# Reordering the first k.v products of a linear-attention and SwiGLU kernel on one core

## Chip, cores and metric

The kernel runs on one core of a Trainium2 chip. The metric is the device time of one execution in microseconds (us), as the median of several executions; lower is better. A profiled execution gives the trace that is read here. The engines are PE (TensorE, matmuls), PEld (its weight loads), DVE (VectorE), ACT (ScalarE), POOL (GpSimd, which here issues most of the loads) and SP (SyncE). "L292" is line 292 of the kernel.

## The reference

```python
def phi(x): return np.where(x > 0, x, np.exp(x) - 1.0) + 1.0
# q, k, v: [batch 8, heads 8, seq 576, dim 64]
kv  = einsum('bhsd,bhse->bhde', phi(k), v)
z   = sum(phi(k), axis=2)
num = einsum('bhsd,bhde->bhse', phi(q), kv)
den = einsum('bhsd,bhd->bhs', phi(q), z)[..., None] + 1e-06
x   = (num / den) as [4608 tokens, 512]
out = (silu(x @ w_gate) * (x @ w_val)) @ w_out        # w_gate, w_val: 512 x 1536
```

## The kernel before

phi(x) is computed as max(x, 0) + min(exp(x), 1). For k, `mx_k` writes the max to `kp`, `exp_k` and `mn_k` write the min to `ek`, and `add_k` adds `ek` into `kp`. The heads of a batch are worked on in two halves (`lp` 0 and 1). `zt` sums k over the sequence on PE, for the max and the min term in turn; `kv_corner` is the k.v product of one half, 36 small matmuls in 64 by 64 tiles; `t_corners` multiplies q by z or by k.v; `lnrd` forms 1/den as exp(-ln(den)) on ACT; `x_t` multiplies the two on DVE; `warm` issues filler matmuls on ones while PE has nothing to do.

```python
WARM = (4, 1, 4, 3, 2, 1, 1, 1)
def kv_corner(b, lp, t, first, last):
    ps = kvp[b]
    for j in range(J):                    # J = 9
        for l2 in range(2):
            for hh in range(2):
                ... nc.tensor.matmul(out=ps[hh][64 x 64 corner], lhsT=t[...], rhs=vr[...],
                                     start=(first and j == 0), stop=(last and j == J - 1))
...                                       # batch 0, the order in which all engines get their work
zt(0, 0, X[1], ek, False, True)
zr_copy(0, 0, X[1])
warm(WARM[4])
t_corners(0, Zr, 0, pp4[2])
lnrd(pp4[2], 0)
q_phi(1, 1, qb)
mn_k(0, 1)
zt(0, 1, Y[0], kp, True, False)
warm(WARM[5])
zt(0, 1, Y[0], ek, False, True)
add_k(0, 0)
zr_copy(0, 1, Y[0])
warm(WARM[6])
kv_corner(0, 0, kp, True, True)
t_corners(0, Zr, 1, Y)
lnrd(Y, 1)
r_copy(0, 0, 1, "VV")
add_k(0, 1)
t_corners(0, R, 0, X)
x_t(0, 0, X)
kv_corner(0, 1, kp, True, True)
r_copy(0, 1, 2, "VV")
warm(WARM[7], ps=pp4[2][1])
l1_mm(0, 0, pp4[2], (0,))                 # layer 1, chunk 0 of x, blocks 0 and 1
l1_mm(0, 1, X, (0,))
t_corners(0, R, 1, pp4[1])
x_t(0, 1, pp4[1])
for c in (1, 2, 3):                       # the other chunks
    l1_mm(0, 0, pp4[2], (c,))
    l1_mm(0, 1, X, (c,))
...
for t in range(4):                        # end of layer 2 of group 0, with batch 1 between
    if t == 1:
        for lp in range(2):
            kv_corner(1, lp, kp, True, True)
        r_copy(1, 0, 2, "VV")
    if t == 2:
        nx(0, dz)                         # q.kv and x of batch 1
        nx(1, cq)
    for fb in range(FO, FB):
        l2_mm(0, t, fb)
```

Every matmul is two PE instructions, a weight load and the matmul itself (the page of before has 2185 of each).

## Time and profile before

| | before |
|---|---|
| median of 3 runs | 314.12 us (313.8 to 314.37) |
| PE busy, share of the span | 98% |
| ACT begins exp of k (first half) | 8.29 us |
| first matmul of L292 (layer 1 proper) | 18.59 us |
| first layer 1 matmul of group 1 | 49.87 us |
| end of the last matmul | 309.02 us |

The trace's clock starts at the span's start. When k lands differs between executions by up to half a microsecond (ACT's first exp of k starts between 7.83 and 8.36 us in the traces of this study) and moves all that follows. So for the first stage I use the interval from that exp to the first matmul of L292: 18.59 - 8.29 = 10.30 us in the kernel before. Its two ends in the ACT and PE timelines of before (start, length, what), and the piece of the chain of waits with chunks 1 to 3 of layer 1:

```profile
8.29 1.16 ACT L120 ACTIVATE ek<-kr 128x1152 f16<-128x1152 f16 x1 [0.27 <-DMA kr<-in_k_dram]
18.59 1.03 PE L292 MATMUL pp<-xT,wg 128*128 128x512 f16 x4
```

```profile
16.01 2.74 PE pp L276 x12
```

### The profile page before, as it was taken

The page shows a single profiled execution, that of the slowest core. Times are in us where ns is not written, and L with a number is a line of the kernel's source. Part 1 is how long each engine was busy: PE and PEld are TensorE (multiplying, and loading weights), DVE is VectorE, ACT ScalarE, POOL GpSimd, SP SyncE. Part 2 cuts the span into 40 slices and gives each one's busy share as a digit, 9 for nine tenths or more (in the row PEclk, how much of TensorE's full clock was granted, in tenths as well). Part 3 has the DMA queues.
Part 4 walks back from the last instruction along what each step waited for, and adds up shares of the span by engine and source line. Part 5 has one row for each costly group of instructions (what it writes and reads, how often), then busy time and mean ns, then how long its engine had stood idle before and what let it go on. Part 6 is the DMA issues. An engine that isn't in the chain of part 4 may idle for free.

```text
span 312.4 us, 5524 instructions
## 1 busy us (share of the span) xinstructions
PE 306.1 (98%) x2185; PEld 142.3 (46%) x2185; DVE 205.0 (66%) x362; ACT 152.8 (49%) x231; POOL 48.6 (16%) x73
## 2 busy tenths in 40 slices
PE   8899999999999999999999999999999999999994
PEld 4344454444544454445444544454444444444442
DVE  4854869999599657976697859874981434143410
ACT  4955959539733845375535643475330333133311
POOL 8655445300000410032001400000000000000000
PEclk9999999999999999999999999999999999999999
DMA  8999999998412594139612990324032300140014
GB/s 215 200 196 200 206 206 236 234 206 140 108 25 41 86 198 118 38 47 188 169 31 47 140 224 4 71 47 92 0 70 58 84 1 1 42 94 0 2 34 101
DMA packets 41178, 32.80 MB, mean 105 GB/s; under 512 B 16448, under 2 KB 36160, under 8 KB 41152
## 3 DMA queue, kind: packets, MB, share of 16 engines
q0 software_dynamic: 20480, 18.29, 37.3%
q1 hardware_dynamic: 20592, 14.13, 18.9%
q8 instruction: 17, 0.28, 0.4%
q14 instruction: 9, 0.07, 0.1%
q10 hardware_dynamic: 80, 0.03, 0.0%
HBM read 37.75 MB, written 9.44 MB: 151 GB/s over the span
## 4 chain that ended last, share of the span: by engine, by line
PE 95%; DMA 2%; DVE 1%; ACT 0%; issue 0%; POOL 0%; POOLq 0%
PE pp L292 57%; PE pp L299 30%; PE pp L276 2%; DMA kr<-in_k_dram 2%; PE pp L185 2%; PE pp L254 2%; PE pp L124 0%; ACT ek L120 0%; PE pp L411 0%; DVE kp L159 0%; PE pp L212 0%; PE pp L374 0%; DVE osb L322 0%; DVE ek L147 0%; DVE R L201 0%
## 5 line engine op out<-in xcount | busy, mean ns | idle before, releaser
L120 ACT ACTIVATE sil<-pp 128x512 f16<-128x512 f32 x108 | 63.5, 597 | 101.8 <-PE pp L292 96.7
L292 PE MATMUL pp<-xT,wg 128*128 128x512 f16 x416 | 106.8, 379 | 0.0
L292 PE MATMUL pp<-xT,wv 128*128 128x512 f16 x416 | 106.8, 379 | 0.0
L285 DVE SCALAR_TENSOR_TENSOR hT<-pp,sil 128x512 f16<-128x512 f32 x108 | 72.3, 681 | 48.5 <-PE pp L292 35.5
L299 PE MATMUL pp<-wo,hT 128*128 128x512 f16 (+2 forms) x444 | 97.1, 374 | 0.6 <-DVE osb L322 0.6
L299 PEld LDWEIGHTS <-hT 128*128 128x128 f16 x444 | 42.0, 98 | 49.8 <-issue 2.1
L292 PEld LDWEIGHTS <-wv 128*128 128x128 f16 x416 | 40.7, 98 | 49.1
L292 PEld LDWEIGHTS <-wg 128*128 128x128 f16 x416 | 40.7, 98 | 48.5
L322 DVE TENSOR_SCALAR osb<-pp 128x512 f32<-128x512 f32 (+1 forms) x19 | 12.9, 681 | 31.3 <-PE pp L299 31.3
L120 ACT ACTIVATE osb<-pp 128x512 f32<-128x512 f32 (+1 forms) x18 | 10.3, 574 | 34.8 <-PE pp L299 34.8
L120 ACT ACTIVATE ek<-kr 128x1152 f16<-128x1152 f16 x16 | 17.9, 1156 | 0.3 <-DMA kr<-in_k_dram 0.3
L120 ACT ACT_TABLE_LOAD x13 | 16.7, 1283 | 2.5 <-PE pp L292 2.4
L706 POOL COPY gate<-qT 128x1 f16<-128x1 f16 x4 | 1.3, 313 | 96.5 <-DMA qT<-qp 68.5
L229 DVE TENSOR_TENSOR qp<-qp,rden 128x1152 f16<-128x1152 f16 x12 | 16.2, 1346 | 0.0
L220 DVE TENSOR_REDUCE den<-prod 128x18 f32<-128x1152 f16 x12 | 16.1, 1342 | 0.0
L120 ACT ACTIVATE eq<-qr 128x1152 f16<-128x1152 f16 (+1 forms) x15 | 15.9, 1102 | 0.0
L271 DVE TENSOR_SCALAR xT<-pp 128x512 f16<-128x512 f32 (+1 forms) x14 | 8.8, 667 | 7.2 <-PE pp L254 7.1
L103 POOL DMA_DIRECT2D vr<-in_v_dram x16 | 12.0, 752 | 8.8 <-DMA wo<-in_moe_w_out_dram 2.4
L103 POOL DMA_DIRECT2D kr<-in_k_dram x16 | 11.5, 723 | 8.4 <-DMA wo<-in_moe_w_out_dram 1.9
L159 DVE TENSOR_TENSOR kp<-ek,kp 128x1152 f16<-128x1152 f16 x16 | 12.1, 757 | 0.5
L103 POOL DMA_DIRECT2D qr<-in_q_dram x14 | 10.2, 730 | 4.8 <-DMA qr<-in_q_dram 1.3
L147 DVE TENSOR_SCALAR ek<-ek 128x1152 f16<-128x1152 f16 x16 | 7.7, 480 | 4.7 <-ACT ek L120 4.5
(83 smaller groups left out, 179.8 us busy)
## 6 DMA issues: line engine op xcount, KB each, us to landing
out_dram<-osb SPq DMA_DIRECT2D x70, 128.0 KB, 3.0
kr<-in_k_dram POOLq DMA_DIRECT2D x16, 288.0 KB, 8.6
vr<-in_v_dram POOLq DMA_DIRECT2D x16, 288.0 KB, 9.9
qr<-in_q_dram POOLq DMA_DIRECT2D x14, 288.0 KB, 11.9
wg<-in_moe_w_gate_dram POOLq DMA_DIRECT2D x5, 256.0 KB, 9.3
wv<-in_moe_w_val_dram POOLq DMA_DIRECT2D x5, 256.0 KB, 9.0
q<-in_q_dram SPq DMA_DIRECT2D x2, 576.0 KB, 4.2
wo<-in_moe_w_out_dram POOLq DMA_DIRECT2D x2, 512.0 KB, 13.0
```

The costliest lines, as they stand in the source:

```text
L103: nc.gpsimd.dma_start(out=dst[b % NB][:, 2 * lp:2 * lp + 2, :], in_=src[b].rearrange("(l a) (c j) d -> (a c) l (j d)", a=2, j=J)[:, 2 * lp ...
L120: nc.scalar.activation(out=out, in_=in_, func=func, bias=bias, scale=scale)
L147: nc.vector.tensor_scalar(out=a, in0=a, scalar1=1.0, scalar2=None, op0=ALU.min)
L159: nc.vector.tensor_tensor(out=a, in0=ek[b % 2][:, lp, :, :], in1=a, op=ALU.add)
L185: nc.tensor.matmul(out=ps[hh][D * l2:D * l2 + D, D * lp:D * lp + D], lhsT=t[b % 2][rows, lp, j, D * l2:D * l2 + D], rhs=vr[b % NB][rows, 2 ...
L220: nc.vector.tensor_reduce(out=den[:, c, :], in_=prod[:, :, :].rearrange("p j (l d) -> p (j l) d", d=D), axis=AX.X, op=ALU.add)
L229: nc.vector.tensor_tensor(out=qv, in0=qv, in1=rden[:, c, :].unsqueeze(2).to_broadcast([P, 2 * J, D]), op=ALU.mult)
L271: nc.vector.tensor_scalar(out=dst, in0=ps[l2][:, c0:], scalar1=1.0 / SC, scalar2=None, op0=ALU.mult)
L285: nc.vector.scalar_tensor_tensor(out=hT[g % 2][:, fb, :], in0=ps[1][:, :], scalar=SC, in1=s[:, :], op0=ALU.mult, op1=ALU.mult)
L292: nc.tensor.matmul(out=ps[h][:, :], lhsT=w[:, c, P * fb:P * fb + P], rhs=xT[g % 2][:, c, :], start=(c == 0), stop=(c == 3))
L299: nc.tensor.matmul(out=l2p[(g, t)][:, n0:n1], lhsT=hT[g % 2][:, fb, P * t:P * t + P], rhs=wo[:, fb, n0:n1], start=(fb == 0), stop=(fb == F ...
L322: nc.vector.tensor_scalar(out=o[:, n0:n1], in0=ps[:, n0:n1], scalar1=1.0 / SC, scalar2=None, op0=ALU.mult)
```

## The change

Its intent: in batch 0, the first half's add, its k.v and the copies of it follow its z at once. The second half's k.v no longer waits for an add, as PE sums it from the max term and the min term. In batch 1, k.v and q.kv each move one tile of layer 2 later, away from banks that ACT is still reading.

```diff
-    WARM = (4, 1, 4, 3, 2, 1, 1, 1)
+    WARM = (4, 1, 4, 4, 2, 2)
...
     lnrd(pp4[2], 0)
+    add_k(0, 0)
     q_phi(1, 1, qb)
+    zt(0, 1, Y[0], kp, True, False)
+    kv_corner(0, 0, kp, True, True)
+    r_copy(0, 0, 1, "VV")
+    warm(WARM[5], ps=X[0])
     mn_k(0, 1)
-    zt(0, 1, Y[0], kp, True, False)
-    warm(WARM[5])
+    t_corners(0, R, 0, X)
     zt(0, 1, Y[0], ek, False, True)
-    add_k(0, 0)
     zr_copy(0, 1, Y[0])
-    warm(WARM[6])
-    kv_corner(0, 0, kp, True, True)
+    x_t(0, 0, X, (0,))
+    kv_corner(0, 1, kp, True, False)
     t_corners(0, Zr, 1, Y)
     lnrd(Y, 1)
-    r_copy(0, 0, 1, "VV")
-    add_k(0, 1)
-    t_corners(0, R, 0, X)
-    x_t(0, 0, X)
-    kv_corner(0, 1, kp, True, True)
+    x_t(0, 0, X, (1,))
+    kv_corner(0, 1, ek, False, True)
     r_copy(0, 1, 2, "VV")
-    warm(WARM[7], ps=pp4[2][1])
...
-            if t == 1:
+            if t == 2:
                 for lp in range(2):
                     kv_corner(1, lp, kp, True, True)
                 r_copy(1, 0, 2, "VV")
-            if t == 2:
+            if t == 3:
                 nx(0, dz)
```

## The prediction

Its "such matmuls" are those of L292, 512 columns in 128*128 tiles, and a "switch" is the change between these and matmuls in 64*64 tiles; the 0.1 us for one is an estimate from its 0.96 and 0.86 us.

> **What bounds the kernel now.** I read the page first, then the chain of waits in order of time, then the timelines of PE, DVE, ACT and POOL for 8 to 19 us and 43 to 62 us, the two stretches that the change touches.
>
> From the page, the busy shares and the summary of the chain:
>
> ```profile
> PE 306.1 (98%) x2185; PEld 142.3 (46%) x2185; DVE 205.0 (66%) x362; ACT 152.8 (49%) x231; POOL 48.6 (16%) x73
> ...
> PE 95%; DMA 2%; DVE 1%; ACT 0%; issue 0%; POOL 0%; POOLq 0%
> ```
>
> The end is set by PE. What another engine does matters only where PE waits for it, or fills a wait with useless work. The chain itself (start, length, what) shows both:
>
> ```profile
> 11.51 0.24 PE pp L124
> 11.74 0.38 PE pp L411 x9
> 12.13 0.24 PE pp L124
> 12.36 0.04 issue
> 12.40 0.55 PE pp L185 x36
> 12.95 0.34 DVE R L201 x2
> 13.29 0.68 DVE kp L159
> 13.97 0.04 issue
> 14.01 0.48 PE pp L185 x36
> 14.49 0.32 PE pp L124
> ...
> 45.72 0.14 PE pp L185
> 45.86 0.01 issue
> 45.88 0.79 PE pp L185 x71
> ```
>
> L124 is a filler matmul on ones, so PE has nothing to do at 11.5, 12.1 and 14.5. L185 is the k.v product: its first half at 12.40 follows DVE work, its second half at 14.01 follows the add of the second half (L159) on DVE. From 14.01 on PE never waits in this stage; the feed-forward matmuls proper (L292) begin at 18.59 by the timeline, and everything after is PE back to back. So the prologue is worth exactly what the start of L292 moves. The third piece, at 45.7, is a stall in layer 2 of group 0: the first k.v matmul of batch 1 is separated from the other 71.
>
> The DVE timeline (start, length) shows why k.v comes late:
>
> ```profile
> 11.23 0.45 DVE L147 TENSOR_SCALAR ek<-ek 128x1152 f16<-128x1152 f16 x1
> 11.60 0.75 DVE L159 TENSOR_TENSOR kp<-ek,kp 128x1152 f16<-128x1152 f16 x1
> 12.26 0.28 DVE L415 TENSOR_SCALAR Zr<-pp 128x128 f16<-128x128 f32 x1
> ...
> 13.21 0.75 DVE L159 TENSOR_TENSOR kp<-ek,kp 128x1152 f16<-128x1152 f16 x1
> ```
>
> The first add waits behind one q operation (10.63) and the min of the second half (11.23), neither of which it needs; the second add stands between the two k.v products.
>
> [...]0.45 us for the min, 0.75 us for the add of the same 1152 elements. Dropping an add is worth more than dropping a min. [...]the trace has 0.86 us for 4 such matmuls (18.59 to 19.45). [...]In the trace 4 matmuls of 512 ahead of a 64-wide product take 0.96 us (44.69 to 45.65), 0.10 more than 0.86, so each switch costs about 0.1 us.
>
> **The change, part 1 (batch 0).** Instructions: one add (0.75 us) leaves DVE; 36 matmuls of k.v join PE, because the second half's k.v is summed from the max and the min term apart. One half costs 0.31 us of PE issue (12.40 to 12.71) plus the mode switch. Fillers stay 17 in all, but one moves ahead of the z product, where PE idled anyway (9.69 to 10.00), and the one at 14.42 (0.23 us) disappears.
>
> Walk from the copy of z at 10.42, which does not move. The durations and gaps are those of before.
> DVE: copy of z 10.42; add of half 0 at 10.63, done 11.38; q operation 11.29 to 11.97; R copies from 11.97 (k.v of half 0 runs 11.43 to 11.91), done 12.33; min of half 1 at 12.24, done 12.69; copy of z of half 1, after its PE sum (12.75 to 13.14), 13.17 to 13.45; x half 0: 13.38 to 14.05 and 13.98 to 14.66; R copies 14.59 to 14.95.
> PE: k.v of half 0 at 11.43 instead of 12.40; two fillers to 12.27; q.kv of half 0 at 12.36; z sum of half 1 at 12.75; its k.v over the max term at 13.1; q.z of half 1 at 13.50 (before 12.71), because it waits for the later copy of z; k.v over the min term at 13.84, ending 14.25 with the switch; then, without a gap, two chunks of layer 1 (0.86, to 15.12), switch and q.kv of half 1 (0.44, to 15.56), chunk 1 (0.86, to 16.42), chunks 2 and 3 (1.73 plus 0.05 of wait), so L292 begins at 18.20.
> Against 18.59 that is 0.39 us. As a sum: PE's unbroken run begins at 13.50 and not 14.01 (-0.51), the filler is gone (-0.23), q.z of half 1 is now inside the run (+0.34): -0.40. The removed add and the added 36 matmuls are not themselves the gain: the add was partly on the path, the matmuls replace fillers and waiting.
>
> **Part 2 (batch 1).** No instruction is added. In before, k.v of batch 1 starts at 45.65 while ACT still reads the same two banks for the logarithm:
>
> ```profile
> 44.56 2.42 ACT L120 ACTIVATE lnt<-pp,epsb 128x512 f32<-128x512 f32 x4 [1.74 <-PE pp L254]
> ```
>
> Four in 2.42 us; the second, which frees the second bank, ends near 45.83, and the chain has the other 71 matmuls from 45.88. The 72 take 0.95 us (45.65 to 46.60), against 0.73 at 73.39 to 74.12, where nothing blocks. One tile later (46.5) the banks have been free for 0.7 us: -0.22 us. The number of mode switches is the same.
> The price is later x of batch 1: q.kv moves behind k.v plus one tile, from 47.57 to about 48.2 on an unshifted clock, so the first x multiply starts near 48.6 (44 to 45 us shows 0.44 from such a product to its reader) instead of 48.28, where it waited for an output copy. Layer 1 of group 1 starts at 49.65, the first x is done at 49.28, the second (0.62 apart) at 49.9 for its use at 50.08: free, by 0.1 to 0.2 us.
>
> Sum: 0.39 + 0.22 = 0.61 us. 314.12 - 0.61 = 313.5 us, 0.2%.
>
> **Rivals.**
> A: ACT becomes the bound of the prologue. Its eight Ln and Exp run without a gap from 11.22 to 16.28 in before, and the last x multiply needs the last of them. They shift by 0.24 with q.z of half 1 (ready 13.95, where ACT is free at 13.71), to 16.52; the last x then ends at 17.23 and is used at 17.33. For: only 0.04 us of slack after the semaphore. Against: both paths hang on the same q.z. If q.z comes another 0.2 later, the gain falls to 0.2: total 313.7.
> B: DMA. Earlier k.v needs v earlier. The POOL timeline, where each issue waits for a landing:
>
> ```profile
> 11.44 0.74 POOL L112 DMA_DIRECT2D wg<-in_moe_w_gate_dram  x1 [0.72 <-DMA vr<-in_v_dram]
> 12.85 0.74 POOL L112 DMA_DIRECT2D wv<-in_moe_w_val_dram  x1 [0.67 <-DMA vr<-in_v_dram]
> ```
>
> The issue view gives 8.3 and 8.9 us from issue (2.88, 3.62) to landing: v at 11.2 and 12.5, wanted at 11.43 and 13.1. It fits by 0.25 us for the first half; should v come 0.3 later, little is lost at once, since two fillers follow. The weights of chunk 0 land near 14.0, wanted at 14.25 and 14.47. Later weights land 1 us or more ahead of use. v of batch 1 lands near 45.0; k.v of it will be wanted at 46.1 instead of 45.65, so part 2 also keeps part 1 from running into that load. If one load binds, 313.7 to 313.9.
> C: part 2 gives its gain back as a wait of layer 1 for x, or DVE falls behind in group 1. DVE is busy without a gap from 48.28 to 55.0 and PE needs the first hidden tile's bank back at 56.78, freed at 55.9: 0.9 us of slack shrinks to about 0.3, since PE comes 0.6 earlier while DVE's absolute time hardly moves. Then the total would be 313.7 to 313.9.
> D: the clock. [...]the page shows 9s throughout and PE's idle gaps become no longer. [...]unlikely.
> E: the chain is as I walked it but the semaphores are slightly faster or slower[...].
>
> **Range and chances.** 0.61 us centre. A, B and C each take up to 0.4 and are one-sided; better than my walk is possible by some 0.3. The three runs of before spread over 0.57 us (313.8 to 314.37), so a median is uncertain by some 0.2. I take 313.05 to 314.1. A 2% change is 6.3 us: the whole prologue up to the first L292 is 18.6 us and most of it is loads and needed work, so faster by 2% is out of reach[...].
>
> **What would show it.** Right: L292 first at 18.1 to 18.3; k.v of half 0 near 11.4, of half 1 in two pieces near 13.1 and 13.8 around q.z; no DVE add at 13.2; the filler before layer 1 gone; k.v of batch 1 as one run of 0.73 us near 46.1; layer 1 of group 1 without a wait, starting near 49.25 instead of 49.87; from there on the same durations, shifted by 0.6. Wrong: L292 at 18.5 or later with a wait of PE on x (rival A) or on a load (B); a wait at L276 near 50 or at L292 near 56 (C); a lower clock row (D). A gain at 18 that shrinks on the way to 300 us would refute the claim that everything after is PE back to back.

## The result, and the profile after

| | before | after |
|---|---|---|
| median of 4 runs | 314.06 us (313.8 to 314.37) | 314.16 us (314.07 to 314.39) |
| ratio of the means | | 1.0004 (95% interval 0.9987 to 1.0021) |
| exp of k to L292 | 10.30 us | 10.67 us |
| L292 to the first layer 1 matmul of group 1 | 31.28 us | 31.07 us |

Ratios here are the mean time of one kernel's fast runs over that of the other's fast runs of the same rounds, so not quite the ratio of the medians.

The expected 0.6 us did not come. The last row shows part 2's 0.21 us; the row above it shows a loss of 0.37 us where a gain of 0.39 was forecast. The two ends of that interval in the timelines after:

```profile
8.10 1.16 ACT L120 ACTIVATE ek<-kr 128x1152 f16<-128x1152 f16 x1
18.77 1.03 PE L292 MATMUL pp<-xT,wg 128*128 128x512 f16 x4
```

The chain of waits after (start, length, what) has the place, and the list of waits for 16 to 18 us gives the same:

```profile
14.08 0.97 PE pp L276 x4
15.05 0.34 PE pp L254 x4
15.39 1.45 PE pp L276 x6
16.84 0.64 issue
17.48 1.46 PE pp L276 x6
...
44.93 1.83 PE pp L299 x8
46.76 0.73 PE pp L185 x72
```

```profile
PE pp L276 <- issue: 0.6, 1, 0.6
```

"Issue" means that PE stood still and waited for nothing that the profile shows. L276 is chunks of layer 1; the twelve matmuls of chunks 1 to 3 ran without a break before (16.01 to 18.75) and are now cut in two. The PE timeline shows where, one matmul a line (start, length, what):

```profile
16.25 0.38 PE L276 MATMUL pp<-xT,wg 128*128 128x512 f16 x1
16.46 0.38 PE L276 MATMUL pp<-xT,wv 128*128 128x512 f16 x1
17.48 0.38 PE L276 MATMUL pp<-xT,wg 128*128 128x512 f16 x1 [0.64 <-issue]
```

These are the first three matmuls of chunk 2. The third reads the same chunk of x as the first two, weights that came in the same transfers, and a bank that it has already summed into; in the trace it has no semaphore to wait for. Its own weight load ran at 16.47, ahead of the gap, so it was not weights that it lacked. Without the gap it would start at 16.68, 0.22 us behind the second, so it loses 0.80 us.

Up to there the walk of the prediction was kept. The k.v of the first half began at 11.25 and q.z of the second at 13.34, which is 0.18 and 0.16 ahead of the walk, with k 0.19 us earlier in this execution. Part 2's line at 46.76 is one run of 72 matmuls in 0.73 us, where before it was split.

What PE lacked has to be something that it needs without a semaphore. The page lists one such thing in its table of DMA queues (packets, MB, share), and the DMA view for 15 to 16.1 us shows one such packet there:

```profile
q8 instruction: 17, 0.28, 0.3%
```

```profile
q8 instruction: 1, 0.02, 5.4%
```

By the name of their queue, those 17 packets of 16 KB carry instructions. In the trace's records the first of them ran from 15.13 to 16.08 us after, and from 15.57 to 16.54 before. If I count PE's records (weight loads, matmuls and the few instructions of its sequencer, two of them ahead of the gap) from the start, the one that stood still is number 449, counted from 0. In the kernel before, number 449 is a matmul of L292 at 25.06 us, because 72 fewer instructions lie ahead of it. The last three packets in the trace after start when PE stands at its records 3736, 3992 and 4248, exactly 256 apart (in the trace before 250 and 252 apart); 4289, a multiple of 256 beyond 449, would be the next boundary. The packets between the first and these are less regular: they start from 41 records ahead of such a boundary to 147 beyond it.

So the new theory, F, which is inferred from these packets and their spacing and named by nothing in the trace: PE's instructions come in blocks of 256, one a packet, and 36 added matmuls, 72 instructions, moved the end of a fetched block from the middle of L292 to the prologue, where PE reached it before the next block had come. (In the trace after, the first packet starts when PE stands at record 436.) The rivals: X, the gap is a wait for x or ACT or another effect of the new order; P, part 2 cost the time; D, the clock. D falls at once: the granted clock was 1.000 in the trace after, and on both sides of the gap the matmuls are about 0.22 us apart.

### The profile page after: what moved, and what is told of

Its sections match the earlier page's. It is cut to its first block, busy times and chain, and to the rows that moved or that the text cites. A ratio compares the mean times of both kernels' runs of the same rounds, so it can differ in the third digit from the quotient of the medians.

```text
span 312.4 us, 5593 instructions
## 1 busy us (share of the span) xinstructions
PE 306.1 (98%) x2221; PEld 142.6 (46%) x2221; DVE 204.4 (65%) x361; ACT 152.8 (49%) x231; POOL 48.4 (15%) x73
## 4 chain that ended last, share of the span: by engine, by line
PE 96%; DMA 2%; issue 0%; DVE 0%; ACT 0%; POOL 0%; POOLq 0%
PE pp L292 57%; PE pp L299 30%; PE pp L276 2%; DMA kr<-in_k_dram 2%; PE pp L254 2%; PE pp L185 2%; PE pp L124 1%; PE pp L411 0%; PE pp L212 0%; PE pp L374 0%; DVE osb L322 0%; DVE kp L143 0%; ACT osb L120 0%; PE pp L538 0%; POOL idx L335 0%
## 5 line engine op out<-in xcount | busy, mean ns | idle before, releaser
L292 PE MATMUL pp<-xT,wg 128*128 128x512 f16 x416 | 106.8, 379 | 0.0
L292 PE MATMUL pp<-xT,wv 128*128 128x512 f16 x416 | 106.8, 379 | 0.0
L292 PEld LDWEIGHTS <-wv 128*128 128x128 f16 x416 | 40.7, 98 | 49.1
L292 PEld LDWEIGHTS <-wg 128*128 128x128 f16 x416 | 40.7, 98 | 48.5
L220 DVE TENSOR_REDUCE den<-prod 128x18 f32<-128x1152 f16 x12 | 16.1, 1344 | 0.0
L159 DVE TENSOR_TENSOR kp<-ek,kp 128x1152 f16<-128x1152 f16 x15 | 11.4, 758 | 0.5
```

The costliest lines, as they stand in the source:

```text
L159: nc.vector.tensor_tensor(out=a, in0=ek[b % 2][:, lp, :, :], in1=a, op=ALU.add)
L220: nc.vector.tensor_reduce(out=den[:, c, :], in_=prod[:, :, :].rearrange("p j (l d) -> p (j l) d", d=D), axis=AX.X, op=ALU.add)
L292: nc.tensor.matmul(out=ps[h][:, :], lhsT=w[:, c, P * fb:P * fb + P], rhs=xT[g % 2][:, c, :], start=(c == 0), stop=(c == 3))
```

## The experiments

### part1_only: batch 0 changed, batch 1 as before

The changed kernel with the last hunk of the diff undone.

> Part 1 alone (batch 0), batch 1 as in the kernel before. Theory F (PE runs out of fetched instructions): the added 36 k.v matmuls, 72 PE instructions, bring the end of a fetched block of instructions to the third matmul of chunk 2 of layer 1, so PE stops there for 0.6 to 1.0 us with no semaphore to wait for, ending near 17.4 us; L292 begins near 18.75 instead of 18.59; total 0.1 to 0.4 us slower than before (314.2 to 314.5). Rival X (the stall is a wait for x or for the last Exp on ACT, rival A of the prediction): the same stall, but it ends when the last x multiply ends, near 17.1. Rival P (part 2 is what cost the time): this run is 0.4 us faster than before.

Measured: 314.6 us median of 5 against 314.11 of 11 (ratio 1.0013, 1.0001 to 1.0025), 0.1 above F's range. In the PE timeline:

```profile
16.80 0.38 PE L276 MATMUL pp<-xT,wv 128*128 128x512 f16 x1
17.73 0.38 PE L276 MATMUL pp<-xT,wg 128*128 128x512 f16 x1 [0.55 <-issue]
```

The gap is there, again ahead of record 449, and ends 1.32 us after the instruction packet (15.46 to 16.41). L292 began at 19.02, later than I wrote, as k came 0.12 us later than in the trace after; exp to L292 is 10.80. Part 1 alone costs half a microsecond, so P falls. X is not yet excluded by this run.

### part2_only: batch 1 changed, batch 0 as before

The kernel before with only the last hunk of the diff.

> Part 2 alone (batch 1), batch 0 as before. Theory F: nothing changes ahead of 44 us, no stall near 17; k.v of batch 1 takes 0.73 us instead of 0.95, layer 1 of group 1 starts 0.2 us earlier relative to L292's first matmul; total 0.2 us faster than before (313.85). Rival P: part 2 gives nothing or costs 0.4 us, as layer 1 waits for x or DVE falls behind.

Measured: 313.99 us median of 5 against 314.11 (ratio 0.9998, 0.9986 to 1.001). The total cannot resolve 0.2 us: single runs went from 313.64 to 314.62. The trace can: L292 to layer 1 of group 1 is 49.42 - 18.35 = 31.07 us against 31.28, and k.v of batch 1 is one piece of 0.73 us in the chain:

```profile
46.35 0.73 PE pp L185 x72
```

So part 2 gives its 0.21 us inside the stage, as predicted; that the total gains it is not shown by this run alone.

### before_plus50: only instructions added, to the kernel before

```diff
+    warm(28, w=8)
     q_turn(0, qa)
...
     warm(WARM[2])
+    warm(22, w=8)
```

> The kernel before with 50 narrow filler matmuls (8 columns[...]) put into two gaps in which PE waits for q (28) and for k (22): 100 more PE instructions, no data dependence and no order of useful work changed. Theory F: the block of instructions now ends 28 instructions ahead of where it ended in the changed kernel, at the first matmul of chunk 0 of layer 1 (14.65 us in before), and PE stands there until about 17.4: 2 to 3 us slower than before (316 to 317), one gap on PE without a semaphore. Rival X, and any theory by which the stall comes from the order of the work, from v, from the weights or from ACT: no gap, at most 0.2 us slower.

Measured: 314.1 us median of 4 against 314.11 (ratio 1.0001, 0.9988 to 1.0014), and no gap, which is what X expected. F's expectation failed as it stood. The trace shows why: the first instruction packet now ran from 11.24 to 12.17, 4.3 us earlier than before (15.57), and record 449, at the place I had named, was reached at 14.38, two microseconds after it. I had kept the transfer at its old time. My reading is that the packet follows PE's own progress: with more instructions early, PE reaches each running number earlier, and the packet came earlier too. As a mark of that progress I take record 129: it ran at 10.17 us before, 9.96 after and 6.93 here, and the packet followed 5.4, 5.2 and 4.3 us later. So I mended F: the packet is set off by how far PE has come, and not at a fixed time. At which record it is asked for no trace shows; 129 is a mark for comparing runs and no more. (The last three packets in the trace after start 41 records ahead of a boundary, 4248 against 4289.)

### after_minus6: six fillers fewer

```diff
-    WARM = (4, 1, 4, 4, 2, 2)
+    WARM = (4, 1, 2, 2, 1, 1)
```

> The changed kernel with six of its 17 fillers of 512 columns left out (4,1,2,2,1,1 in place of 4,1,4,4,2,2): 12 PE instructions fewer, the order of all useful work kept. Theory F: the block of instructions ends 12 instructions later, at the first matmul of L292, which PE reaches near 18.1 when the next block is there (17.4): no gap, L292 begins near 18.1 to 18.2, total 0.5 to 0.7 us faster than before (313.4 to 313.6). Rival X: the gap near 16.7 stays, total as the changed kernel (314.1). Rival D (clock): matmuls of 512 columns take longer than 0.216 us apart somewhere after 11 us, total above 315.

Measured: six runs at 315.6, 315.5, 314.15, 315.7, 313.4 and 313.16 us. The profiled one (315.6) has no gap at record 449 (20.23), but the clock fell and PE came there late, so this is no test of F. The page's row of the granted clock, and the PE timeline:

```profile
PEclk9689999999999999999999999999999999999999
```

```profile
15.16 0.61 PE L276 MATMUL pp<-xT,wg 128*128 128x512 f16 x1
15.57 0.63 PE L276 MATMUL pp<-xT,wv 128*128 128x512 f16 x1
```

The matmuls are 0.41 us apart in place of 0.22, and the records of the clock have it at one half from 10.92 to 17.75 us. Rival D was dismissed in the prediction as unlikely; with six fillers fewer the granted clock was 0.989 to 0.995 in four of six runs (of the 33 runs of the kernel before in the rounds of these experiments, one is that low: 0.995, 315.78 us). Only one of the four has a trace. From 1.06 us, where PE begins, to the fall at 10.92 its PE timeline has no idle stretch over 0.80 us (ahead of 8.79), but PE was busy for only 0.86 of the 2.00 us from 8 to 10; in the trace after, which kept its clock, it was 1.81. Whether such short gaps set off the fall no run isolates. The two runs whose granted clock was 1.0 took 313.4 and 313.16 us, at or below the 313.4 to 313.6 that F expected, but two runs without a profile show nothing of the gap.

### after_again: the changed kernel once more

Nothing edited; in the same rounds as the next two.

> The changed kernel once more, on the chip and in the rounds of the runs beside it. Theory F as mended by the last runs ([...]the transfer [...]takes about 1 us, and PE goes on some 1.35 us after its end): the gap ahead of the third matmul of chunk 2 again, ending 1.3 to 1.4 us after the end of that transfer; total 314.0 to 314.4.

Measured: 314.34 us median of 6 against 314.1 of 11 (ratio 1.0001, 0.9989 to 1.0013). The gap is ahead of record 449 again and ends at 17.48, 1.51 us after the packet (15.02 to 15.97); exp of k to L292 took 10.73 us. So the gap belongs to the kernel and not to one execution.

### after_plus14: 28 instructions more, in the wait for k

```diff
     warm(WARM[2])
+    warm(14, w=8)
```

> The changed kernel with 14 narrow fillers more in the gap in which PE waits for k: 28 more PE instructions. Theory F: the block ends 28 instructions of useful work earlier, so the gap moves from the third matmul of chunk 2 to the first matmul of chunk 0 (near 14.0), at the same running number of PE instructions; [...]the transfer starts near 13.5 to 14.3 and PE goes on near 16 to 16.6: a gap of 1.8 to 2.6 us in place of 0.8, total 1.0 to 1.8 us over the changed kernel (315.1 to 316). Theories of order, x, ACT or weights: the gap stays where it was, total within 0.2 of the changed kernel.

Measured: 317.54 us median of 4 against 314.1 (ratio 1.0097, 1.0077 to 1.0118). The PE timeline:

```profile
13.48 0.51 PE L185 MATMUL pp<-vr,ek 64*64 64x64 f16 x36
16.71 0.38 PE L276 MATMUL pp<-xT,wg 128*128 128x512 f16 x1 [2.72 <-issue]
```

The gap moved to the first matmul of chunk 0, exactly the instruction that was named, which is again record 449. The packet ran from 14.24 to 15.18; the gap ends 1.53 us later. No useful work was moved, so a theory of order, of x, of ACT or of weights cannot place it there. X falls. Nor is it the number 449 alone: in before_plus50, with the packet early, PE passed it in the prologue without a stop. The loss is larger than expected for a second reason: PE stood for 2.8 us, and the clock was at one half for 3.4 us after it (records of the clock), which is about half of the loss: the first matmul of chunk 0 to L292 took 5.48 us (16.71 to 22.19), against 3.94 before (14.65 to 18.59).

### after_gated: fewer loads queued

All loads behind v are issued only after POOL has copied an element of the first half's z:

```diff
-    ld_w1(0, 256, 0, 2)
-    ...                                    # all loads up to ld2(v, vr, 1)
...
     warm(WARM[4])
+    nc.gpsimd.tensor_copy(out=gate[:, :], in_=Zr[0][:, 0, 0, 0:1])
+    ld_w1(0, 256, 0, 2)
+    ...                                    # the same loads in the same order
     t_corners(0, Zr, 0, pp4[2])
```

> The changed kernel with every load behind v held back until the copy of z of the first half is written (near 10.3 us)[...]. Theory F with the delay put down to the queued loads: the instruction transfer starts near 12 to 13.5 us and not at 15.1, and no gap without a semaphore stands at the 449th PE instruction; instead PE waits for the weights of layer 1 and the total is 1 to 3 us longer. If the 5 us are a fixed delay of the instruction fetch and not the loads, it still starts near 15.

Measured: one run, 316.96 us, state unknown (granted clock 1.0). The instruction packet ran from 12.11 to 13.25, 2.4 us after record 129 (9.71) instead of 5.2, which is the 5 us of the expectation. No gap stands at record 449 (18.68). PE waits for weights instead, as the waits for 13 to 19 us show:

```profile
PE pp L276 <- DMA wv<-in_moe_w_val_dram: 0.9, 1, 0.9
PE pp L276 <- DMA wg<-in_moe_w_gate_dram: 0.8, 1, 0.8
```

So, by this one execution, more than half of the 5 us goes when the loads are held back. Holding the loads back is no cure, since PE then waits for them.

### split_add: part of the add on DVE, part on PE

In the trace after, DVE is idle for 0.48 us between the min of the second half and its copy of z. The add of 5 of the 9 column groups fits there; PE sums only the other 4 from two terms. (The hunks that define `add_part` and give `kv_corner` its two limits of j are left out.)

```diff
     zt(0, 1, Y[0], ek, False, True)
+    add_part(0, 1, 5)                        # add_k for j = 0..4
     zr_copy(0, 1, Y[0])
     x_t(0, 0, X, (0,))
-    kv_corner(0, 1, kp, True, False)
+    kv_corner(0, 1, kp, True, False, 5, J)   # j = 5..8
+    warm(1, ps=Y[1])
     t_corners(0, Zr, 1, Y)
     lnrd(Y, 1)
     x_t(0, 0, X, (1,))
-    kv_corner(0, 1, ek, False, True)
+    kv_corner(0, 1, kp, False, False, 0, 5)
+    kv_corner(0, 1, ek, False, True, 5, J)
```

> The changed kernel, but the second half's add is done on DVE for 5 of 9 column groups, in DVE's idle time ahead of the second copy of z, and only the other 4 are summed from two terms: 20 k.v matmuls fewer, one filler more ahead of q.z of the second half, so 38 PE instructions fewer ahead of L292. Theory F: the block ends 38 instructions later, inside L292 near 20 to 21 us, long after the transfer (restart near 17.4): no gap, L292 begins near 18.1, total 313.2 to 313.6, 0.5 to 0.9 faster than before. Any theory in which the gap comes from the new order of the work (x, ACT, v, the banks): the gap stays near 16.7, total 314.0 to 314.4. If the clock drops in some executions as it did with six fillers fewer, those are above 315.

Measured: 313.67 us median of 6 against 314.1 of before and 314.34 of the changed kernel in the same rounds (ratio to before 0.9983, 0.9969 to 0.9997), just above F's range. The PE timeline at the place of the gap, where the line numbers are 4 higher:

```profile
16.84 0.38 PE L280 MATMUL pp<-xT,wv 128*128 128x512 f16 x1
17.05 0.38 PE L280 MATMUL pp<-xT,wg 128*128 128x512 f16 x1
```

There is no gap; record 449 is inside L292, at 21.18, well after its packet (15.54 to 16.51). Exp of k to L292 took 10.02 us, 0.28 less than before. The granted clock was 0.997 or more in all six runs.

### after_plus50: the changed kernel with 100 instructions more

The same edit as in before_plus50.

> The changed kernel with the same 50 narrow fillers (100 PE instructions) in the same two gaps as the run on the kernel before. Theory F as mended: [...]the transfer runs near 11.2 to 12.2 and PE can go on from about 13.55; the block now ends 100 instructions of useful work earlier, near the q.z product of the second half, which PE reaches near 13.35: a gap of 0.1 to 0.3 us there in place of 0.8 near 16.7, so that MORE instructions make it faster: 313.5 to 313.9, 0.3 to 0.7 below the changed kernel. If only the number of instructions counted, it would be slower than the changed kernel, as with 14.

Measured: 314.32 us median of 6 (313.84 to 315.41) against 314.11 (ratio 1.0003, 0.998 to 1.0025). In the total this is a miss, and it is inconclusive. In the trace the gap is gone: the packet ran from 11.30 to 12.27, and record 449, a weight load of the second half's k.v, ran at 13.70 without a wait. Instead the second half's k.v waited for v:

```profile
13.38 0.48 PE L185 MATMUL pp<-vr,kp 64*64 64x64 f16 x36 [0.35 <-DMA vr<-in_v_dram]
```

Exp of k to L292 took 10.51 us, 0.16 less than after and still 0.21 more than before: the added fillers also held back the first sum over k, which began 0.97 us behind the exp (0.52 in the trace after). Layer 1 of group 1 began at 49.41, 0.43 earlier than after, of which 0.27 is an earlier k, and the last matmul ended at 308.56 against 308.95. But the last two stores of this execution took 3.0 and 3.2 us to land, against 1.9 and 2.1 after. So its span of 313.0 is longer although its matmuls were done sooner. Why the stores were slow is open. The trace has one candidate that no other has: an 18th packet of instructions, from 308.69 to 310.35, beside these stores. PE's records pass number 4545 (449 + 16 x 256) in this kernel alone, which fits F; that the packet slowed the stores is not shown.

### full_add: the add back on DVE whole

```diff
     zt(0, 1, Y[0], ek, False, True)
+    add_k(0, 1)
     zr_copy(0, 1, Y[0])
...
-    kv_corner(0, 1, kp, True, False)
+    warm(2, ps=Y[1])
...
-    kv_corner(0, 1, ek, False, True)
+    kv_corner(0, 1, kp, True, True)
```

> The changed kernel with the whole add of the second half back on DVE (between its min and its copy of z), its k.v in one piece behind q.z, and two fillers where the max term's k.v stood: 68 PE instructions fewer ahead of L292. Theory F: no gap; but the add (0.68 us) overfills DVE's idle time of 0.48 and holds the copy of z back by 0.2 us, so L292 begins 0.2 later than with the split add: 313.7 to 313.9, 0.2 slower than the split add and still faster than both kernels. If it is as fast as the split add, the two-term sum buys nothing at all.

Measured: 313.55 us median of 6 against 314.11 (ratio 0.998, 0.9961 to 0.9998), a little below F's range. The DVE timeline:

```profile
12.51 0.76 DVE L159 TENSOR_TENSOR kp<-ek,kp 128x1152 f16<-128x1152 f16 x1
13.19 0.28 DVE L415 TENSOR_SCALAR Zr<-pp 128x128 f16<-128x128 f32 x1
```

The copy of z starts 5.12 us after the exp of k (8.07), in the trace after 4.89 (12.99 - 8.10): the add does hold it back by 0.23 us. Exp of k to L292 took 10.13 us, 0.11 more than with the split add. In the total the two cannot be told apart (313.55 and 313.67, in different rounds). So the two-term sum buys 0.1 us at best where it is used for 4 groups. Used for all 9, it costs a gap of 0.8.

## Why the prediction was wrong

It said 313.5 us, 313.05 to 314.1; the median was 314.16.

**Right: the walk of DVE and ACT.** The last Exp ended at 16.37 and the last x multiply began at 16.40, where the walk had 16.52 and 16.55, with k 0.19 us earlier. Rival A, ACT as the bound of the prologue, did not come true: PE could have gone on with the stalled matmul at 16.68, and the last x is needed only two matmuls further, by chunk 3.

**Wrong: "chunks 2 and 3 (1.73 plus 0.05 of wait), so L292 begins at 18.20".** This is the step that failed, the end of the run that was to be "without a gap". Up to chunk 1 it held; chunks 2 and 3 took 2.52 us (16.25 to 18.77) in place of 1.78. The sum behind it (13.50 + 0.34 + 0.41 + 0.86 + 0.44 + 0.86 + 1.78 = 18.19, rounded on the way to 18.20) has no term for PE's supply of instructions. From 16.68 with the remaining six matmuls, and chunk 3 not before the last x (17.09 plus 0.06), L292 would have begun at 18.01 in the trace after by calculation, 9.91 us after the exp of k, which would have been the 0.39 us forecast. It began at 18.77: 0.76 us lost. With it the claim that "the matmuls replace fillers and waiting" fell: the 36 matmuls cost little in PE time, but they are 72 instructions. The kernel with nearly the same order and fewer instructions (split_add) had 0.28 us in the stage, and after_plus14 moved the gap by instructions alone.

**Wrong: no rival for it.** Five rivals were named and none was this. The page before already had the sign, 17 packets on a queue of instructions; by the trace, the first of them ran in a stretch with DMA busy throughout (9 in every slice of the DMA view of before for 15.5 to 16.6 us, 200 GB/s). Rival D, the clock, was no part of it (granted 1.000 in the trace after); where the clock was at one half for 3.4 us (after_plus14), that cost about 1.5.

**Right: part 2, in mechanism and size.** The stall on ACT's logarithm is gone, 0.73 in place of 0.95 us, and the stage is 0.21 us shorter (the totals cannot resolve that); layer 1 of group 1 began with no wait for x (rival C did not come true).

**Right: everything after is PE back to back.** From layer 1 of group 1 to the last matmul took 259.15 us before (49.87 to 309.02) and 259.11 after (49.84 to 308.95).

**Rival B** (a load binds) did not come true in the trace after: k.v of the first half had no wait for v. In after_plus50 k.v of the second half waited 0.35 us for v, so its slack is small.

The balance of the two traces: +0.37 in the first stage (-0.39 forecast, +0.76 by the gap), -0.21 by part 2, -0.19 because k came earlier in that execution: -0.03 at layer 1 of group 1, which is what stands there (49.84 against 49.87).

**Open.** Why PE goes on only 1.3 to 1.5 us after the packet's end, in the four traces with a gap alike (1.32, 1.40, 1.51 and 1.53). At which record a block is asked for: from the mark at record 129 to the packet's start there are 5.1 to 5.5 us in nine traces, 4.3 and 4.4 in the two with 50 narrow fillers, and 2.4 with fewer loads queued. That these packets are PE's and not another engine's is inferred: only PE has instructions for 17 blocks of 256 (4453 of the 5593 in the trace after; the other engines have 1140 together), the last packets are 256 PE records apart, the gap stands ahead of record 449 in three kernels, and only the kernel that passes number 4545 has an 18th packet. The trace does not name the engine.

## What to carry to other kernels

A PE wait marked "issue" with no semaphore, at the same running number of PE instructions in each variant, can be a late block of instructions, as is inferred here (gaps of 0.8 us, in after_plus14 of 2.8); look for the instruction packets in the DMA view. Where DMA is as busy as here (9 in every slice of the DMA view of after for 8 to 18 us) and small matmuls follow one another as quickly (36 of k.v in 0.31 us), count PE instructions as well as PE time: here 20 matmuls fewer, worth almost nothing in PE time, turned no gain into about half a microsecond (split_add, 313.67 against 314.1 of before; the changed kernel had 314.34). Fillers are not free to remove either: with six fewer the granted clock fell in four of six executions (0.989 to 0.995), in the traced one to a half for 6.83 us.
